# Four global phases, a Strassen step in the second products too, 768-token blocks

## Chip, core, metric

One core of one Trainium2 chip. The metric is the device time of one execution in microseconds (us). Engines: TensorE (PE) multiplies matrices, VectorE (DVE), ScalarE (ACT) and GpSimd (POOL) work element by element, SyncE (SP) issues the DMAs. DRAM tiles are written and read back by DMA.

## What is computed

A linear attention with RMS norm, then two feed-forward layers on 4608 tokens of width 512; all in float32, with weights in float64 words that the kernel converts itself.

```python
kv = einsum('bhsd,bhse->bhde', k, v)          # 8 batches, 8 heads, 576 tokens, 64
out = einsum('bhsd,bhde->bhse', q, kv)
x = out / sqrt(mean(out**2) + 1e-6) * g_norm   # -> [4608, 512]
h = x @ w_in                                   # layer 1: 512 -> 2048
x = (max(h, 0) + alpha * min(h, 0)) @ w_out    # 2048 -> 512
y = ((x @ w_a) * (x @ w_b)) @ w_out2           # layer 2: 512 -> 1536 -> 512
```

## The kernel before

Every operand of the layers is split into two float32r parts, high and low (a `copy` that rounds on ACT, and a subtraction on DVE), and every product is three matmuls: high x low, low x high, high x high.

*First products* (`x @ w_in`, `x @ w_a`, `x @ w_b`): a unit is 256 columns of a weight. One Strassen step (the Winograd form) makes 7 products out of 8 blocks of 256 x 256: `Unit.combine` prepares 7 weight combinations, `X.operands` 7 combinations of a token block of 512 (columns of a matmul: HB = 256). `first` runs a pair of units: 7 products x 2 units x 6 matmuls = 84 matmuls (L583) into the PSUM banks A to D; `copy` (ACT, L598) and `add` (DVE, L602) take the results into H, then the prelu (L624 to L626) or the product a * b (L630), and the split into g (L633 ACT, L634 DVE).

*Second products* (`@ w_out`): `second` multiplies g at once by `WUnit`s, without a Strassen step, 512 columns a matmul (L652), into the four banks acc0 to acc3.

There are four passes over all 9 blocks: half of layer 1 twice, half of layer 2 twice. A pass visits each block with 2 or 3 pairs, each with both products. The first half of a layer stores its partial sums (x2p, outp), the second half loads them and adds (L665, L669). So 90 pairs run, with 7560 matmuls of 256 and 3024 of 512 columns.

*Attention* has 16 steps (`Step`): `kv` (L420, L421), `out` (L437, L442), `norm` (squares L462 on ACT, sums L464, some small instructions on DVE, scaling L481 on POOL), `tr` (transposes L491, L495, then ACT, then a store to xd). Two half-batches make a batch of 576 tokens. The transposes of steps 0 and 1 go from PSUM straight into the first block's operand `xs0.x`. Five steps come ahead, the other 11 one per pair.

*Weights*: `to_float` turns words into float32 (L213 ACT, L214 to L218 DVE, L220 POOL). The first pass's units are converted straight away (`direct`); the others are converted in an earlier pass, stored (`wd`) and loaded again (`build`: `combine` L337, split L295, L296) when a tile of theirs is free.

*Order*: no loop order runs. Every instruction group is a task with a price (COST, AFTER), a priority (a time) and its dependences; `Plan.order` takes for each engine the ready task of lowest priority value, and the kernel is written out in that order. Each engine and the DMA queue of SP work strictly in it.

Of the kernel before, what the change touches and what calls it, by code (L numbers as in the profile page):

```python
# [22 lines left out]
BLK = 512  # L23
CH = 112
NB = TOK // BLK
HB = BLK // 2
EPS = 1e-6

# [5 lines left out]
NFIRST = 5  # L34
AHEAD = 1e6


STEP_AT = [-7.4, -4.8, -4.45, -3.65, -12.5]
X_AT = -0.4
FETCH_AT = [-17.8, -12.9, 7]  # L40
UNIT_AT, WUNIT_AT = [-6.65, -2.75], [0.15, 21.5]

REST_AT, NEXT_X_LOAD, NEXT_X, BUILD, CONVERT = -2, 1.6, -0.3, 6.6, AHEAD
LAST_THREE, SECOND = 0.28, [0.6, 0.1]
SPREAD = [(0, 11), (0, 7), (2, 8)]
# [3 lines left out]
COST = {"v": lambda n: 0.075 + 1.11e-3 * n, "v2": lambda n: 0.075 + 0.556e-3 * n, "a": lambda n: 0.124 + 1.03e-3 * n,  # L49
        "p": lambda n: 0.122 + 2.56e-3 * n, "t": lambda n: n / 2400, "d": lambda n: max(0.5, n / 318e3)}  # L50
AFTER = {"v": 0.13, "a": 0.14, "p": 0.2, "t": 0.2, "d": 2.7}

# [101 lines left out]
def body(ctx: ExitStack, tc, kvm, kvt, qt, gn, w_in, alpha, w_o1, w_a, w_b, w_o2, outT):  # L154
# [24 lines left out]
    x2p = [in_dram([P, 4, BLK], f"x2p{b}") for b in range(NB)]  # L179
    x2d = [in_dram([P, 4, BLK], f"x2d{b}") for b in range(NB)]  # L180
    outp = [in_dram([P, 4, BLK], f"outp{b}") for b in range(NB)]

# [6 lines left out]
    wpool = ctx.enter_context(tc.tile_pool(name="w", bufs=1))  # L189
    spool = ctx.enter_context(tc.tile_pool(name="stg", bufs=1))  # L190
    xpool = ctx.enter_context(tc.tile_pool(name="x", bufs=1))
    hpool = ctx.enter_context(tc.tile_pool(name="h", bufs=1))
# [3 lines left out]
    late = []  # L196

    def sb(pool, shape, tag, n=1, dt=F32):
        return plan.ring(tag, n, lambda key: pool.tile(shape, dt, tag=key, name=key))

    def bank(tag, shape):
        return plan.ring(tag, 1, lambda key: psum.tile(shape, F32, tag=key, name=key))
# [20 lines left out]
    class Built:  # L223


        def __init__(self, w, f0, need):
            self.w, self.f0, self.need, self.closed, self.dram = w, f0, need, False, None

        def take(self):

            n = {"unit": 6, "wu": 4}[self.tag]
            i = plan.counts.get(self.tag, 0)
            plan.counts[self.tag] = i + 1
            key = f"{self.tag}{i % n}"
            self.key = key
            self.pool = (lambda: late[0]) if key in ("unit4", "unit5") else (lambda: wpool)

        def make(self, shape, dt):
            old = plan.rings.get(self.key)
            b = Buf(lambda: self.pool().tile(shape, dt, tag=self.key, name=self.key), old.tasks if old else ())  # L240
            if self.key in ("unit4", "unit5") and not old:
                b.before = list(attention)
            plan.rings[self.key] = b
            return b

        def cuts(self, t, o=0):
# [57 lines left out]
    class Unit(Built):  # L304
# [15 lines left out]
        def place(self):  # L320
            self.c = sb(spool, [P, 8, 2, P], "stg", 2)
# [512 lines left out]
```

## Time and profile before

| | |
|---|---|
| median of 3 runs | 1740.4 us (1740.27 to 1740.61) |
| the profiled execution | 1740.45 us, its span 1738.7 us |
| PE busy | 1695.9 us, 98% |
| DVE busy | 1249.5 us, 72% |
| ACT busy | 769.0 us, 44% |
| POOL busy | 155.0 us, 9% |
| DMA | 195.83 MB, mean 113 GB/s |

The busy time is that of one profiled execution; matmuls overlap in their ends, so the mean duration of one is longer than the distance from one to the next. The chain of waits follows the work that ended last backwards. "L652" is a line of the kernel above.

### The profile page before, as it was taken

The page shows a single profiled execution, that of the slowest core. Times are in us where ns is not written, and L with a number is a line of the kernel's source. Part 1 is how long each engine was busy: PE and PEld are TensorE (multiplying, and loading weights), DVE is VectorE, ACT ScalarE, POOL GpSimd, SP SyncE. Part 2 cuts the span into 40 slices and gives each one's busy share as a digit, 9 for nine tenths or more (in the row PEclk, how much of TensorE's full clock was granted, in tenths as well). Part 3 has the DMA queues.
Part 4 walks back from the last instruction along what each step waited for, and adds up shares of the span by engine and source line. Part 5 has one row for each costly group of instructions (what it writes and reads, how often), then busy time and mean ns, then how long its engine had stood idle before and what let it go on. Part 6 is the DMA issues. An engine that isn't in the chain of part 4 may idle for free.

```text
span 1738.7 us, 28280 instructions
## 1 busy us (share of the span) xinstructions
PE 1695.9 (98%) x11384; PEld 1569.6 (90%) x11384; DVE 1249.5 (72%) x1969; ACT 769.0 (44%) x1315; POOL 155.0 (9%) x110
## 2 busy tenths in 40 slices
PE   4799999999999999999999999999999999999999
PEld 4789989989999999999999999999999999999998
DVE  7997778677667889887786677765577566566654
ACT  4566665665566555555553333333244222222221
POOL 3432122120000001110000111100000000000000
PEclk9899999999999999999999999999999999999999
DMA  9755565442133434443231343321023222221112
GB/s 275 216 167 172 169 204 169 155 145 77 49 96 123 134 122 146 137 135 110 101 114 69 107 134 107 107 98 46 29 85 122 74 74 73 74 66 57 57 41 73
DMA packets 101491, 195.83 MB, mean 113 GB/s; under 512 B 11760, under 2 KB 36336, under 8 KB 99056
## 3 DMA queue, kind: packets, MB, share of 16 engines
q1 hardware_dynamic: 101360, 194.03, 34.3%
q8 instruction: 89, 1.46, 0.3%
q14 instruction: 42, 0.34, 0.1%
HBM read 133.18 MB, written 60.82 MB: 112 GB/s over the span
## 4 chain that ended last, share of the span: by engine, by line
PE 94%; DVE 3%; DMA 1%; issue 1%; SPq 0%; POOL 0%; ACT 0%; POOLq 0%
PE acc L652 39%; PE A L583 15%; PE C L583 15%; PE D L583 14%; PE B L583 7%; PE A L420 1%; PE B L437 1%; DMA kvm<-in_kvm_dram 1%; PE A L437 1%; DMA unit<-in_w_in_dram 0%; PE C L442 0%; DVE H L602 0%; DVE wu L218 0%; PE acc L420 0%; PE A L421 0%
## 5 line engine op out<-in xcount | busy, mean ns | idle before, releaser
L652 PE MATMUL acc<-g,wu 128*128 128x512 f32 x3024 | 714.4, 392 | 3.7 <-DVE g L634 3.7
L652 PEld LDWEIGHTS acc<-g,wu 128*128 128x128 f32 x3024 | 559.1, 188 | 113.4 <-DVE g L634 4.3
L583 PE MATMUL D<-xc,unit 128*128 128x256 f32 x2160 | 291.1, 284 | 5.1 <-DVE xc L568 3.6
L583 PE MATMUL A<-xc,unit 128*128 128x256 f32 x2160 | 289.8, 284 | 0.0
L583 PE MATMUL C<-xc,unit 128*128 128x256 f32 x2160 | 288.2, 283 | 0.3 <-DVE H L602 0.3
L583 PEld LDWEIGHTS A<-xc,unit 128*128 128x128 f32 x2160 | 278.7, 192 | 7.4
L583 PEld LDWEIGHTS D<-xc,unit 128*128 128x128 f32 x2160 | 272.2, 191 | 5.8 <-DVE xc L568 3.8
L583 PEld LDWEIGHTS C<-xc,unit 128*128 128x128 f32 x2160 | 271.4, 191 | 1.6 <-DVE H L602 0.7
L598 ACT COPY H<-A 128x512 f32<-128x512 f32 x180 | 105.2, 585 | 337.7 <-PE A L583 330.4
L633 ACT CAST g<-H 128x512 fp32r<-128x512 f32 x252 | 155.5, 622 | 208.3 <-DVE H L630 119.5
L634 DVE TENSOR_TENSOR g<-H,g 128x512 fp32r<-128x512 f32 x252 | 183.2, 734 | 48.0 <-ACT g L633 45.2
L602 DVE TENSOR_TENSOR H<-H,C 128x512 f32<-128x512 f32 x180 | 123.4, 686 | 81.6 <-PE C L583 77.0
L568 DVE TENSOR_TENSOR xc<-xf,xc 128x512 fp32r<-128x512 f32 x143 | 104.0, 730 | 88.9 <-ACT xc L567 88.0
L567 ACT CAST xc<-xf 128x512 fp32r<-128x512 f32 x144 | 89.1, 620 | 166.1 <-PE A L583 111.1
L602 DVE TENSOR_TENSOR H<-H,B 128x512 f32<-128x512 f32 x90 | 61.7, 686 | 119.4 <-PE B L583 119.1
L220 POOL TENSOR_TENSOR stg<-stg 128x512 f32<-128x512 f32 x52 | 74.8, 1438 | 805.3 <-DVE stg L218 521.7
L602 DVE TENSOR_TENSOR H<-H,D 128x512 f32<-128x512 f32 x180 | 123.2, 685 | 31.8 <-PE D L583 25.4
L583 PE MATMUL B<-xc,unit 128*128 128x256 f32 x1080 | 143.6, 282 | 0.0
L626 DVE SCALAR_TENSOR_TENSOR H<-H,nal_sb,t 128x512 f32<-128x512 f32 x144 | 116.7, 810 | 34.1 <-ACT H L625 34.0
L583 PEld LDWEIGHTS B<-xc,unit 128*128 128x128 f32 x1080 | 135.3, 191 | 0.0
L624 ACT ACTIVATE t<-H 128x512 f32<-128x512 f32 x144 | 90.8, 631 | 74.5 <-DVE H L626 39.0
L625 ACT ACTIVATE H<-H 128x512 f32<-128x512 f32 x144 | 90.8, 630 | 2.4
(94 smaller groups left out, 1227.5 us busy)
## 6 DMA issues: line engine op xcount, KB each, us to landing
xf<-x2d SPq DMA_DIRECT2D x18, 1024.0 KB, 4.8
kvm<-in_kvm_dram SPq DMA_DIRECT2D x32, 448.0 KB, 5.9
wd<-stg SPq DMA_DIRECT2D x52, 256.0 KB, 2.2
stg<-in_w_o_dram SPq DMA_DIRECT2D x20, 512.0 KB, 4.0
q<-in_qt_dram SPq DMA_DIRECT2D x32, 288.0 KB, 3.8
x2p<-y SPq DMA_DIRECT2D x36, 256.0 KB, 2.5
y<-x2p SPq DMA_DIRECT2D x36, 256.0 KB, 4.3
x2d<-y SPq DMA_DIRECT2D x36, 256.0 KB, 2.1
```

Of the source, the lines that this page charges most:

```text
L220: task("p", n, lambda: nc.gpsimd.tensor_add(out(), permute(f32(a())), permute(f32(u()))), prio, [A, U], [dst])
L567: task("a", 512, lambda c=c, v=v: nc.scalar.copy(c.t[:, 0], v()), prio, r, [(c, 0)])
L568: sub(512, lambda e, c=c, v=v: e.tensor_sub(c.t[:, 1], v(), f32(c.t[:, 0])), prio, r + [(c, 0)], [(c, 1)])
L583: nc.tensor.matmul(bk.t[:, u], w[:, a, i, kk, :], c[:, b, kk, :], start=bool(new and u == 0 and kk == 0 and m == 0), stop=(kk == 1 and m = ...
L598: task("a", 512, lambda: nc.scalar.copy(H.t[:, :, q], bk.t), k, [(bk, 0), (bk, 1)], [(H, (0, q)), (H, (1, q))])
L602: task("v", 512, lambda: nc.vector.tensor_add(H.t[:, :, q], H.t[:, :, p], bk.t), k, [(bk, 0), (bk, 1), (H, (0, p)), (H, (1, p))], [(H, (0, ...
L624: task("a", 512, lambda t=t, v=v: nc.scalar.activation(t.t, v(), AF.Relu), pk, pv, [(t, 0)])
L625: task("a", 512, lambda v=v: nc.scalar.activation(v(), v(), AF.Relu, scale=-1.0), pk, pv, pv)
L626: task("v", 512, lambda t=t, v=v, nal=nal: nc.vector.scalar_tensor_tensor(v(), v(), nal, t.t, ALU.mult, ALU.add), pk, pv + [(t, 0)], pv)
L633: task("a", 512, lambda g=g, v=v: nc.scalar.copy(g.t[:, 0], v()), pk, pv, [(g, 0)])
L634: sub(512, lambda e, g=g, v=v: e.tensor_sub(g.t[:, 1], v(), f32(g.t[:, 0])), pk, pv + [(g, 0)], [(g, 1)], "v")
L652: nc.tensor.matmul(a_.t, w.h.t[:, a, i % 2, d * P:(d + 1) * P], g.t[:, b, :], start=(start and m == 0), stop=(stop and m == 2))
```

## The change

Layer by layer, all first products of all blocks run, and then all second products: four phases. In between, g stands in DRAM (`gd`), unsplit; partial sums x2p and outp are gone. First products take blocks of 768 tokens (6 blocks; matmuls of 384 columns) and use five PSUM banks, each group of six matmuls writing one bank; two banks gather two or three products, so ACT copies 8 and DVE adds 6 results of 384 columns per pair. Layer 1's first phase visits six blocks with four pairs of units each, but begins with three pairs of blocks 0, 1 and 2 (list `V`); layer 2's goes over the blocks twice with three pairs. Second products take 512 tokens (9 blocks) and units of 256 rows, by a Strassen step: per unit two loads from `gd`, four differences of 256 columns (L599), one split of 1,792 columns (L605 ACT, L606 DVE), 7 x 6 = 42 matmuls of 256 columns (L613). Each of the seven products gathers over all units in a bank of its own; after the last unit one copy and seven sums on DVE (L626) make the block's four quarters. So there are 5040 matmuls of 384 and 5292 of 256 columns.

The buffers share memory: a token block lies in F0, H in F1 and F2, and in the second phases these three hold the loaded g; `rops` holds the seven split operands of a block, or three units of g. All units lie in eight tiles w0 to w7; w6 and w7 lie where attention's buffers were, and are first written after attention's last instruction. Six units are converted at the start (w0 to w5, three pairs). Four attention steps come ahead; two more go with each of the first six pairs. Transposes always go through xd, and q has two buffers and not three. Splits and differences go to DVE alone.

```diff
-BLK = 512
+T1ST, N1 = 768, 384
+T2ND, N2 = 512, 256
-NFIRST = 5
+NFIRST = 4
...
-    x2p = [in_dram([P, 4, BLK], f"x2p{b}") for b in range(NB)]
-    outp = [in_dram([P, 4, BLK], f"outp{b}") for b in range(NB)]
+    gd = [[in_dram([P, 2, TOK], f"gd{la}_{u}") for u in range(n)] for la, n in ((0, 8), (1, 6))]
...
+    SLOTS = [f"w{i}" for i in range(8)]
+    def slot(key, shape, dt):
+        old = plan.rings.get(key)
+        b = Buf(lambda: (late[0] if key in SLOTS[6:] else pool).tile(shape, dt, tag=key, name=key),
+                old.tasks if old else (attention if key in SLOTS[6:] else ()))
...
+    def first(k, la, units, js, x):
...
+        for u in range(2):
+            copy(u, 0, X_[u], prod(u, 0, X_[u], 1))
+        for u in range(2):
+            prod(u, 2, Y_[u], 1)
+            copy(u, 1, X_[u], prod(u, 1, X_[u], 0))
+        for u in range(2):
+            Z_[u] = bank("b4", [P, 512])
+            add(u, 0, Z_[u], prod(u, 4, Z_[u], 1))
+            t = prod(u, 3, X_[u], 0)
+            copy(u, 3, X_[u], t)
+            add(u, 3, Y_[u], t)
+        for u in range(2):
+            copy(u, 2, X_[u], prod(u, 6, X_[u], 0))
+            add(u, 1, Y_[u], prod(u, 5, Y_[u], 0))
...
+    ORDER = [0, 1, 3, 6, 2, 5, 4]
+
+    def second(k, la, b, j, n, unit, bk):
+
+        g, t0 = gd[la][j], b * T2ND
+        s = sb(["F0", "F1", "F2"], [P, 8, N2])
...
+        for i, o in enumerate((lambda: s.t[:, 0::7], lambda: s.t[:, 4:6])):
+            dma(262144, o, lambda i=i: g.t[:, i, t0:t0 + T2ND].rearrange("p (h t) -> p h t", h=2), k - 16,
...
+        for o, a, c in ((t1, b12, b11), (t2, b22, t1), (t3, b22, b12), (t4, b21, t2)):
+            sub(N2, lambda e, o=o, a=a, c=c: e.tensor_sub(s.t[:, o[0]], s.t[:, a[0]], s.t[:, c[0]]), k - 7,
...
+        c = rop((plan.counts.setdefault("gx", 0) % 3) * 14 * N2, 14 * N2)
...
+        task("a", 7 * N2, lambda: nc.scalar.copy(half(0), s.t[:, 0:7]), k - 7, reads, [(c, 0)])
+        sub(7 * N2, lambda e: e.tensor_sub(half(1), s.t[:, 0:7], f32(half(0))), k - 7, reads + [(c, 0)], [(c, 1)], "v")
...
+        copy(0, 0)
+        add(1, 0, 1)
+        add(2, 1, 3)
+        add(3, 2, 2)
+        add(2, 2, 6)
+        add(1, 1, 2)
+        add(1, 1, 5)
+        add(0, 0, 4)
...
+    V = [(0, 0, [0, 1, 2]), (0, 1, [0, 1, 2]), (0, 2, [0, 1, 2, 3]), (0, 0, [3]), (0, 3, [0, 1, 2, 3]), (0, 1, [3]),
+         (0, 4, [0, 1, 2, 3]), (0, 5, [0, 1, 2, 3])]
+    V += [(0, b, None) for b in range(NB2)]
+    V += [(1, b, [3 * h, 3 * h + 1, 3 * h + 2]) for h in range(2) for b in range(NB1)]
+    V += [(1, b, None) for b in range(NB2)]
```

How PE's order stands where attention runs among the products, before (L420, L421 are kv, L437 the output, L491 and L495 the transposes of a step; L583 and L652 products):

```order
L491 MATMUL B<-ident,o_120 128x112 x4
L420 MATMUL A<-kvm_2828 128x128 x4
L421 MATMUL A<-kvt_2848 128x128
L420 MATMUL A<-kvm_2858 128x128 x4
L421 MATMUL A<-kvt_2871 128x128
L583 MATMUL C<-xc_2826,unit_267 128x256 x6
L583 MATMUL D<-xc_2856,unit_240 128x256 x6
L437 MATMUL A<-kvbd,q_2762 112x128 x4
L491 MATMUL C<-ident,o_120 128x112 x4
L583 MATMUL D<-xc_2856,unit_267 128x256 x6
L652 MATMUL acc_2653<-g_2904,wu_1244 128x512 x3
L652 MATMUL acc_2660<-g_2904,wu_1244 128x512 x3
```

Between two pieces of attention stand products. In the changed kernel this is so for nine visits of pairs; then, at the end of attention (L276 kv of step 15, L346 and L350 transposes, L292 and L297 the output, L537 a first product; w_2789 is unit 6):

```order
L276 MATMUL b_2657<-kvt_2555 128x128
L346 MATMUL b_2705<-ident,o_108 128x112 x4
L346 MATMUL b_2715<-ident,o_108 128x112 x4
L350 MATMUL b_2720<-ident,o_108 128x128 x2
L292 MATMUL b_2723<-kvbd,q_2680 112x128 x4
L292 MATMUL b_2733<-kvbd,q_2685 112x128 x4
L297 MATMUL b_2740<-kvbd,q_2680 128x128
L297 MATMUL b_2740<-kvbd,q_2685 128x128
L346 MATMUL b_2764<-ident,o_109 128x112 x4
L346 MATMUL b_2771<-ident,o_109 128x112 x4
L350 MATMUL b_2776<-ident,o_109 128x128 x2
L537 MATMUL b_2795<-rops,w_2789 128x384 x6
```

The transposes of step 14, the output of step 15 and its transposes follow one another without a product between them, and the next product reads unit 6.

DVE's order late in the kernel before, about one pair of layer 2 (L602 results of the first products, L630 and L634 g, L337 and L296 a unit being built):

```order
L602 TENSOR_TENSOR H_12885<-H_12885,B 128x2x256
L602 TENSOR_TENSOR H_12885<-H_12885,C 128x2x256
L602 TENSOR_TENSOR H_12885<-H_12885,D 128x2x256
L337 TENSOR_TENSOR stg_12901<-stg_12901 128x256 x2
L602 TENSOR_TENSOR H_12885<-H_12885,C 128x2x256
L337 TENSOR_TENSOR stg_12901<-stg_12901 128x256
L630 TENSOR_TENSOR H_12885<-H_12885 128x512
L602 TENSOR_TENSOR H_12885<-H_12885,D 128x2x256
L337 TENSOR_TENSOR stg_12901<-stg_12901 128x256
L634 TENSOR_TENSOR g_12974<-H_12885,g_12974 128x512
L630 TENSOR_TENSOR H_12885<-H_12885 128x512
```

The same engine in the changed kernel in layer 1's second products, where a block ends:

```order
L606 TENSOR_TENSOR rops<-F_5753,rops 128x1792
L599 TENSOR_TENSOR F_5841<-F_5841 128x256
L606 TENSOR_TENSOR rops<-F_5779,rops 128x1792
L626 TENSOR_TENSOR y_5900<-t,b_5471 128x512
L599 TENSOR_TENSOR F_5841<-F_5841 128x256
L626 TENSOR_TENSOR y_5917<-y_5900,b_5479 128x512
L626 TENSOR_TENSOR t<-t,b_5490 128x512
L626 TENSOR_TENSOR y_5934<-y_5917,b_5515 128x512
L626 TENSOR_TENSOR y_5900<-y_5900,b_5515 128x512
L626 TENSOR_TENSOR y_5917<-y_5917,b_5507 128x512
L626 TENSOR_TENSOR y_5900<-y_5900,b_5526 128x512
L599 TENSOR_TENSOR F_5841<-F_5841 128x256 x2
```

The seven sums of a block stand together, between the subtractions (L606) and differences (L599) that the next units wait for.

More of the change, by code (lines that the diff above doesn't have):

```diff
@@ L187, in body @@
     nal_sb = const.tile([P, DF1 // P], F32, name="nal_sb")
[L189 to L192, printed above, removed]
+    pool = ctx.enter_context(tc.tile_pool(name="main", bufs=1))
     psum = ctx.enter_context(tc.tile_pool(name="ps", bufs=1, space=bass.MemoryType.PSUM))
@@ new lines, in body @@
+    attended(lambda: steps[NFIRST - 1].tr(TR0))
+    for i in range(3, 6):
+        us1[i].fetch(SLOTS[i], 25.0 + 8 * (i - 3))
+        owner[SLOTS[i]] = us1[i]
+    x = X(0, 0)
+    x.load(26.0)
+    x.operands(32.0)
+    for i in range(6):
+        us1[i].direct(us1[i].need - 6, 2 if i < 2 else 1)
+    rest = us1[6:] + wo1 + [u for p in us2 for u in p] + wo2
+    rest.sort(key=lambda u: u.need)
+    convs, builds = list(rest), list(rest)
+    due = {}
+    for i, u in enumerate(rest):
+        if u in us1:
+            due[u] = START + 40 + 25 * i
+        elif u in wo1:
+            due[u] = START + 140 + 25 * wo1.index(u)
+        elif u in wo2:
+            due[u] = wo1[0].need + 420 + 40 * wo2.index(u)
+        else:
+            due[u] = wo1[0].need + 8 + 32 * (rest.index(u) - rest.index(us2[0][0]))
@@ new lines, in body @@
+    end = None
+    pending = [i for i in sorted(at_time)]
+    trq = []
+    for pi, (vi, j, t) in enumerate(pieces):
+        la, b, ps = V[vi]
+        fst = pi == 0 or pieces[pi - 1][0] != vi
+        if ps is not None:
+            units = (pairs1, us2)[la][j]
+            end = first(t, la, units, [2 * j, 2 * j + 1] if la == 0 else [j], x)
+        else:
+            n = 8 if la == 0 else 6
+            units = [(wo1, wo2)[la][j]]
+            if fst:
+                bk = [bank(f"b{i}", [P, 2, N2]) for i in range(7)]
+            end = second(t, la, b, j, n, units[0], bk)
+        for u in units:
+            if last[u] == pi:
+                u.closed = True
+        if pi + 1 < len(pieces) and pieces[pi + 1][0] != vi and V[vi + 1][2] is not None:
+            x = X(V[vi + 1][0], V[vi + 1][1])
+            tn = pieces[pi + 1][2]
+            x.load(tn - 30)
+            x.operands(tn - 9)
+        for i in [i for i in pending if at_time[i] == pi]:
+            pending.remove(i)
+            attend(i, t + 6.0 * (i % 2) - 4)
+            st = steps[-1]
+            attended(lambda: st.kv("b7"))
+            if trq:
+                p_ = trq.pop()
+                attended(lambda: p_.tr(TR0))
+            attended(lambda: (st.out(TR0), st.norm()))
+            trq.append(st)
+        if not pending and trq:
+            p_ = trq.pop()
+            attended(lambda: p_.tr(TR0))
+        while convs and due[convs[0]] <= t:
+            u = convs.pop(0)
+            u.convert(t + CONVERT, [end])
+        while builds and builds[0] not in convs:
+            u = builds[0]
+            free = [s for s in SLOTS if (s in owner and owner[s].closed) or
+                    (s not in owner and not pending and not trq)]
+            if not free:
+                break
+            key = min(free, key=lambda s: last[owner[s]] if s in owner else -1)
+            u.build(key, u.need - BUILD)
+            owner[key] = u
+            builds.pop(0)
@@ L782, in body @@
+    assert not convs and not builds
     make_identity(nc, ident)
```

688 lines of the change are left out of this document (294 added, 394 removed).

## The prediction

> **What bounds the kernel now.** I read the chain of waits first, then the time by stage.
>
> ```profile
> PE 94%; DVE 3%; DMA 1%; issue 1%; SPq 0%; POOL 0%; ACT 0%; POOLq 0%
> PE acc L652 39%; PE A L583 15%; PE C L583 15%; PE D L583 14%; PE B L583 7%; PE A L420 1%; PE B L437 1%; DMA kvm<-in_kvm_dram 1%; PE A L437 1%; DMA unit<-in_w_in_dram 0%; PE C L442 0%; DVE H L602 0%; DVE wu L218 0%; PE acc L420 0%; PE A L421 0%
> ```
>
> TensorE's matmuls are 94% of the chain: second products (L652) 39%, first products (L583) 51%. The stages show where that holds (columns: stretch, length, then busy time of each engine with its instructions, granted clock, DMA share, GB/s):
>
> ```profile
> core 0: us, PE busy (x) PEld busy (x) DVE busy (x) ACT busy (x) POOL busy (x), PEclk, DMA share, GB/s
> 0.00:40.00 40.00, 19.36 (x110) 18.00 (x110) 31.26 (x55) 16.56 (x26) 13.45 (x17) 0.96 0.95 276
> 80.00:120.00 40.00, 34.77 (x238) 32.09 (x237) 37.79 (x65) 25.30 (x50) 14.66 (x10) 0.91 0.56 183
> ...
> 700.00:800.00 100.00, 100.00 (x642) 91.36 (x641) 88.04 (x137) 54.66 (x95) 10.07 (x7) 1.00 0.47 153
> 660.00:680.00 20.00, 20.00 (x125) 17.99 (x125) 19.18 (x29) 12.63 (x22) 3.01 (x3) 1.00 0.57 191
> ```
>
> PE is idle only at the start. Later it is full, even where VectorE (DVE) is 88% busy, and for 20 us 96%. So what counts is PE time per product, PE's idle start, and whether DVE stays under PE. The price of a matmul comes from the chain in order of time (start, length):
>
> ```profile
> 1631.28 5.47 PE acc L652 x24
> 1677.70 5.47 PE acc L652 x24
> 1724.12 10.92 PE acc L652 x48
> ```
>
> 24 matmuls of 512 columns take 5.47, so 0.2279 us each. The block between the first two rows is 46.42 us long and holds 3 x 24 of these and 3 x 84 of 256 columns: (46.42 - 16.41)/252 = 0.1191 each. The last ends at 1735.04, 3.7 us before the span's end: the tail. All products are 7560 x 0.1191 + 3024 x 0.2279 = 1589.6 us. Attention on PE:
>
> ```profile
> 10.89 2.07 PE L420 MATMUL acc<-kvm 112*128 112x128 f32 x8 [10.89 <-DMA kvm<-in_kvm_dram]
> ...
> 56.30 1.63 PE L583 MATMUL A<-xc,unit 128*128 128x256 f32 x6
> ...
> 69.56 2.67 PE L583 MATMUL D<-xc,unit 128*128 128x256 f32 x12 [3.61 <-DVE xc L568]
> ...
> 76.59 0.55 PE L491 MATMUL acc<-ident,o 112*128 112x112 f32 x4
> 76.98 0.39 PE L495 MATMUL acc<-ident,o 128*128 128x128 f32 x2
> 77.20 1.06 PE L420 MATMUL A<-kvm 112*128 112x128 f32 x8
> ...
> 78.31 1.04 PE L437 MATMUL acc<-kvbd,q 128*112 128x128 f32 x8
> 79.19 1.06 PE L420 MATMUL A<-kvm 112*128 112x128 f32 x8
> ...
> 80.31 0.61 PE L442 MATMUL acc<-kvbd,q 128*128 128x128 f32 x4
> 80.67 0.95 PE L583 MATMUL C<-xc,unit 128*128 128x256 f32 x6
> ...
> 118.85 0.61 PE L442 MATMUL C<-kvbd,q 128*128 128x128 f32 x4
> ```
>
> From start to start: a kv half 1.11, an output half 0.88, the rest of the output 0.36, a transposed half 0.39, the last transposes 0.22. A step is 2 x (1.11 + 0.88 + 0.39) + 0.36 + 0.22 = 5.34 us, 16 steps 85.4. Span 1738.7 less products and attention leaves 63.7 us of idle and slow clock.
>
> **The change, part by part.** The sum is against the span; the profiled execution took 1740.45, 1.75 more, and agrees with the median of 1740.4.
>
> *Products.* First products: 60 block-and-pair visits x 84 = 5040 matmuls of 384 columns, a width without a row. Bounds by proportion: 384/512 x 0.2279 = 0.1709 and 384/256 x 0.1191 = 0.1787. I take the mean of the two rows, 0.1735, since 384 lies midway: 874.4 us. Second products: 126 unit visits x 42 = 5292 of 256 columns, 630.3. Sum 1504.7, which is 84.9 less than now; 13 less or 26 more at the bounds.
>
> *Start.* Now the first product runs at 56.30, once two steps are done, from an operand that the transposes write directly. Afterwards a block takes 768 tokens, so steps 0 to 3 must pass through DRAM first. Before that load the queue carries four steps (1.77 MB each), five units of raw weights and stores, some 13.5 MB: at the 276 GB/s of the first row 49 us from about 4. Then the second part of the load, one difference, one cast and one subtraction: steady products from about 74 us (69.56 now). PE's work until then is four steps, a kv and two products, 25.6: idle 48, with ends 40 and 64 (a start at 90, if step 3 is held up by weight conversions as today).
>
> *Nine visits and twelve steps, then a gap.* PE's new order has 9 visits (131 us) mixed with steps 4 to 15; it then has no product until units 6 and 7 are built, whose tiles lie where attention's buffers were. The last transposes, output, norm and transposes stand one after the other. Price of a norm:
>
> ```profile
> L462 ACT ACTIVATE sq<-o 128x640 f32<-128x640 f32 x32 | 23.7, 740 | 5.2 <-DVE sm L464 5.1
> L464 DVE TENSOR_REDUCE sm<-sq 128x10 f32<-128x640 f32 x32 | 26.0, 812 | 10.6 <-ACT sq L462 10.4
> ```
> ```profile
> 131.07 2.93 POOL L481 TENSOR_TENSOR o<-o,sm 128x640 f32<-128x640 f32 x2 [7.33 <-DVE sm L476]
> ```
>
> From the output of 118.85 (end 119.46) to the scaling at 131.07 it takes 11.6 under load; two squares and one sum alone are 2.3. I take 8, with the engines emptier, plus 2.9 for the scalings. Step 14: 8 + 2.9 + 0.6 = 11.5; copies and output of step 15: 2.7; its norm and transposes 11.5; cast and subtraction of 1,792 columns, by L296's row below 2 each: 4. About 30, less PE's own 6.3 and some 4 of overlapping halves: idle 20, ends 8 and 27. I add 6 for waits inside the nine visits. After pauses the clock is low:
>
> ```profile
> 50.00:55.00 5.00, 2.58 (x11) 2.23 (x12) 4.94 (x6) 0.63 (x1) 5.00 (x4) 0.50 1.03 243
> 55.00:60.00 5.00, 5.00 (x28) 5.00 (x27) 5.00 (x11) 2.55 (x7) 1.66 (x1) 0.53 0.79 273
> ```
>
> Half clock over some 5 us of work after each of three pauses, with little PE work in two: 4 us. The Trainium skill (TensorE: Matmul & The Clock Gate, "Part 1: The HAM clock gate") says that about 3.4 us without matmuls brings the half clock back, for about 3.4 us. That speaks against a change that opens a gap; by its figures three pauses cost 5 us, one more than my sum has, and the two rows agree.
>
> *DVE.* The prices (busy, mean ns) and the spacing:
>
> ```profile
> L602 DVE TENSOR_TENSOR H<-H,C 128x512 f32<-128x512 f32 x180 | 123.4, 686 | 81.6 <-PE C L583 77.0
> L626 DVE SCALAR_TENSOR_TENSOR H<-H,nal_sb,t 128x512 f32<-128x512 f32 x144 | 116.7, 810 | 34.1 <-ACT H L625 34.0
> L215 DVE SCALAR_TENSOR_TENSOR stg<-stg 128x512 int32<-128x512 int32 x52 | 45.5, 875 | 1.1
> L218 DVE SCALAR_TENSOR_TENSOR stg<-stg 128x512 f32<-128x512 uint32 x52 | 37.7, 725 | 1.0
> L296 DVE TENSOR_TENSOR unit<-stg,unit 128x1792 fp32r<-128x1792 f32 x18 | 36.4, 2022 | 3.4 <-ACT unit L295 3.2
> L337 DVE TENSOR_TENSOR stg<-stg 128x256 f32<-128x256 f32 x80 | 33.5, 433 | 1.6 <-POOL stg L220 1.2
> L214 DVE TENSOR_SCALAR stg<-stg 128x512 int32<-128x512 int32 x52 | 24.7, 475 | 19.4 <-ACT stg L213 18.8 <-DMA wd<-stg 0.4
> L217 DVE TENSOR_SCALAR stg<-stg 128x512 int32<-128x512 int32 x52 | 23.7, 455 | 0.7
> ```
> ```profile
> 53.78 1.75 DVE L568 TENSOR_TENSOR xc<-t,xc 128x512 fp32r<-128x512 f32 x1
> ...
> 59.88 0.68 DVE L562 TENSOR_TENSOR xf<-xf 128x512 f32<-128x512 f32 x1
> 60.48 0.68 DVE L562 TENSOR_TENSOR t<-xf,t 128x512 f32<-128x512 f32 x1
> ```
> ```profile
> 53.27 1.71 POOL L220 TENSOR_TENSOR stg<-unit 128x512 f32<-128x512 f32 x1
> ```
>
> Neighbours start 0.60 apart and last 0.68, so 0.08 of each overlaps. Second products of layer 1: per unit four differences of 256 (L337) and one subtraction of 1,792 (L296), 3.75; 72 units are 270. With 56 sums of 512 (38), ten weight conversions (20 halves at 2.53, 51) and 12 of remainder: 371, less 0.08 on 505 instructions: 331. PE needs 360.5. Beside a POOL addition a DVE instruction took 1.75 and not 0.69; 20 such additions fall here: 21 more at most, 352. That is 92 to 98%, in the order of the 88 and 96% above where PE lost nothing: I put 4 us of waits, ends 0 and 31 (392 without overlap). The 15 last visits of layer 1's first products are tighter: 55 prelu instructions of 768 columns (1.5 x 0.810), 8 conversions, 7 builds and the operands are 234, less 23 for overlap, up to 16 for POOL: 211 to 227 against 218.6 of PE. I put 8, ends 0 and 31. Layer 2's first products have 426 against 525, its second 249 against 270: no loss. ACT has 116 instructions against DVE's 505 in the second products: hidden under DVE.
>
> *Borders, DMA, tail.* Between first and second products, the last prelu, its store and the new operand share ACT and DVE: one more chain of cast (2.0) and subtraction (2.0) stands bare: 5 us; the other two borders together 3. Intermediate g goes through DRAM, 66 MB each way, and the partial sums leave it: in the second products 0.52 MB per 5 us and the rest, some 175 GB/s, under the 276 of the first row. Tail 4, as now.
>
> Sum: 1504.7 + 85.4 + idle (48 + 6 + 20 + 4 + 8 + 5 + 4 + 3 + 4 = 102) = 1692 of span, **1694 us**.
>
> **Rivals.** *DVE becomes the bound.* For it: the high ends above, 250 against 218.6 and 392 against 360.5, and every new DVE instruction has two inputs. Against it: 96% in the row of 660 to 680 with PE at 20.00. Halfway to the high ends it is +25, 1719; at the ends +50, 1744. The Trainium skill (SBUF — State Buffer, "Who interferes with whom") says that a DVE instruction with two SBUF inputs and a GpSimd instruction that reads SBUF lock each other out for a whole instruction; the rows of 53.27 and 53.78 agree. By it 20 additions of 1.71 would take 34, not 21, from DVE: 365 against 360.5, 5 us more in my sum.
>
> *Attention sets the early time.* Its start at 90 and norms of 11.6: +16 and +7, 1717; a little more with waits between steps, 1725. For it: norms of 11.6 under load. Against it: conversions now come behind attention.
>
> *The operand loop of the second products sets the pace (slower than before).* Three tiles F hold a unit each from load to subtraction:
>
> ```profile
> y<-x2p SPq DMA_DIRECT2D x36, 256.0 KB, 4.3
> ...
> wu<-in_w_o_dram SPq DMA_DIRECT2D x8, 512.0 KB, 8.7
> ```
>
> Load 4.3, four differences 1.4, cast and subtraction 4: 9.7, and three tiles cover 3 x 5.0 = 15. It decides above 15, and those 5.3 us also cover a load that stands on SP's queue behind the store of a converted weight half, which waits for POOL. From a loop of 16.1 (0.37 more on each of 126 units, 46 us) the kernel is slower than now: a load of 10.7. At 12 us the loop is 17.4, 5.8 a unit: +100, 1794. Against it: 4.3 for the same size, and 8.7 only for twice the size in the crowded start.
>
> *384 columns cost 0.1787*: +26, 1720.
>
> **How the numbers follow.** Forecast as worked out (1660 to 1715) 0.60; DVE 0.20; attention 0.10; operand loop 0.06; width 0.04. The range 1660 to 1735 reaches low to a short gap and no waits (-12 - 18), high to the DVE case short of its end. Within 0.2% (3.5 us, about what this kernel's runs can tell apart) 0.03, the edge of the DVE case; slower 0.09: the loop, and DVE at its end; faster 0.88.
>
> **What would show it.** Right: 384-column matmuls spaced 0.173 and 256-column 0.119; steady products from 74 us; a hole of 20 to 25 us with four attention pieces near 270 to 290; PE near 100% and DVE 90% and more in the second products. Wrong: PE waiting for the F tiles' subtractions all along, or DVE at 100% with PE below 95%.

## The result, and the profile after

The changed kernel takes 1834.55 us (median of four; three lie at 1830.25 to 1834.58) where the kernel before takes 1740.34: a ratio of 1.0534, 95% interval 1.0513 to 1.0554. It is 5.3% slower; forecast were 1694 us and a gain. One execution took 4375 us and one of the last version below 2060 us, for reasons that stay open: no ratio counts them, and as the profiler recorded the first, the profile after is of a second run of the same kernel.

> The changed kernel once more, unchanged, for a profile of an ordinary execution (the profiled one took 4375 us with matmuls of 256 columns 0.298 us apart; the others 1830 to 1835 us at a granted clock of 0.952). Theory 1 (the granted clock): matmuls stand closer than before and PE is nearly always busy, but the clock falls below 1.00 for long stretches; 0.048 of 1832 us, some 88 us, is lost there, and the rest of the time is near my sum. Theory 2 (waits): the low mean clock is only that of pauses, PE is idle for 100 us and more beyond the 102 that I counted, in the first products of layer 1 or the second products, where DVE or the operand loop is late. Theory 3 (width): a matmul of 384 columns costs more than 0.1787 us at clock 1.00.

It took 1830.53 us (ratio 1.0522, interval 1.0504 to 1.0540). Its chain of waits, by engine and by line:

```profile
PE 80%; DVE 11%; ACT 3%; issue 3%; DMA 2%; POOL 0%; SPq 0%; DVEq 0%; ACTq 0%; POOLq 0%
PE b L537 45%; PE b L613 32%; PE b L292 2%; DVE rops L606 1%; DVE F L576 1%; PE b L275 1%; DVE rops L505 1%; DVE w L460 1%; DVE stg L451 1%; PE b L346 1%; ACT w L458 1%; DVE F L599 1%; ACT t L574 1%; DMA kvm<-in_kvm_dram 1%; DVE F L547 1%
```

PE was 94% of the chain and is 80%. No single line takes its place: some fifteen lines have about 1% each. That is the picture of many different waits, not of one new bound. The unbroken stretches of the chain give the price of the products (start, length, matmuls):

```profile
629.86 266.56 PE b L613 x2230
...
1036.17 279.74 PE b L537 x1601
...
1320.64 223.11 PE b L537 x1284
...
1563.23 258.48 PE b L613 x2172
```

384 columns cost 279.74/1601 = 0.1747 and 0.1738 us, 256 columns 0.1195 and 0.1190. With 0.174 and 0.1192 all products are 877.0 + 630.8 = 1507.8 us; forecast were 1504.7. The saving in matmuls is there in full. The loss is in the rest, and the stages tell where. I cut at the first product, the end of attention, the first second product, layer 2's first product and its first second product (columns: stretch, length, busy time of each engine with its instructions, clock, DMA share, GB/s):

```profile
core 0: us, PE busy (x) PEld busy (x) DVE busy (x) ACT busy (x) POOL busy (x), PEclk, DMA share, GB/s
0.00:71.20 71.20, 33.09 (x191) 30.96 (x191) 45.27 (x89) 29.96 (x54) 24.38 (x24) 0.80 0.83 255
71.20:319.50 248.30, 214.91 (x1365) 209.60 (x1366) 172.06 (x301) 166.56 (x295) 50.95 (x33) 0.91 0.61 202
319.50:592.20 272.70, 234.56 (x1246) 227.73 (x1244) 214.10 (x303) 189.48 (x294) 24.02 (x16) 0.93 0.48 169
592.20:983.20 391.00, 368.81 (x3043) 366.59 (x3043) 339.14 (x512) 149.50 (x115) 51.57 (x20) 0.97 0.52 170
983.20:1543.60 560.40, 534.46 (x3027) 530.35 (x3026) 397.28 (x576) 237.89 (x405) 23.62 (x16) 0.97 0.35 123
1543.60:1828.80 285.20, 271.85 (x2269) 271.24 (x2267) 219.76 (x331) 93.45 (x62) 0.00 (x0) 0.98 0.41 131
```

Lost is a stage's length less its matmuls at the prices above (and 85.4 for attention). Third row: 272.70 - 1246 x 0.174 = 55.9. The last column is the best version of the experiments, shown at their end.

| stage | work, after | lost, forecast | lost, after | lost, last version |
|---|---|---|---|---|
| start and attention | 216 | 78 | 103 | 86 |
| last 15 visits of layer 1's first products | 217 | 8 | 56 | 19 |
| border and second products, layer 1 | 364 | 9 | 27 | 14 |
| border and first products, layer 2 | 526 | 2 | 34 | 7 |
| border, second products, tail | 270 | 5 | 15 | 16 |
| sum | 1593 | 102 | 235 | 142 |

Of the 235 us PE stands idle for 1828.8 - 1657.7 = 171 (the span less the busy time of all stages), where 98 were forecast. In the other 64 it works, but slower than the price. The slow clock is enough for that: the granted clock of the stages is 0.80 to 0.98, and their busy times, each times what its clock lacks to 1, sum to some 75 us, an estimate from these rounded figures. So of the three theories ahead of this run, waits have the larger part and the clock the rest; a dear matmul has none. Some rows of PE alone (stretch, length, busy time, clock, DMA share, GB/s), then the matmuls behind three pauses, which stand in brackets:

```profile
416.00:418.50 2.50, 2.33 (x13) 1.00 0.28 112
452.00:456.00 4.00, 4.00 (x15) 0.58 0.35 100
475.00:478.00 3.00, 3.00 (x10) 0.50 0.86 292
511.00:514.00 3.00, 3.00 (x10) 0.50 0.75 250
```
```profile
416.17 4.44 PE L537 MATMUL b<-rops,w 128*128 128x384 f32 x24 [2.29 <-ACT F L544]
451.75 17.46 PE L537 MATMUL b<-rops,w 128*128 128x384 f32 x90 [2.36 <-ACT F L544]
508.95 1.31 PE L537 MATMUL b<-rops,w 128*128 128x384 f32 x6 [2.42 <-ACT F L544]
```

After the pause of 2.29 us the clock is full. After one of 5.59 us (shown below) PE runs at half clock for some 5 us (the next 16 matmuls take 5.38 us and not 2.8): the pause is paid twice. But pauses of 2.36 and 2.42 us, with shorter ones close by (1.16 and 1.05 us before the one, 0.47 after the other), end in 3 us of half clock too. The Trainium skill (TensorE: Matmul & The Clock Gate, "Part 1: The HAM clock gate") gives about 3.4 us as the idle time that brings the half clock. The pauses of 2.29 and 5.59 us agree with that and those of 2.36 and 2.42 us do not; here the measurement decides.

**The start.** PE alone, cut where the steady products begin and around the hole at attention's end:

```profile
0.00:95.39 95.39, 49.63 (x290) 0.80 0.76 231
95.39:295.90 200.51, 190.55 (x1226) 0.96 0.66 218
295.90:324.38 28.48, 8.94 (x43) 0.61 0.28 111
```

Steady products come at 95 us and not at 74. But PE is busy for 49.6 us before them and not for 25.6, so it idles for 45.8 us there, then for 10.0 and 19.5; forecast were 48, 6 and 20. The excess of this stage is slow work: of its 103 us, 319.5 - 33.1 - 214.9 = 71.5 are idle, and some 31 are work above the price.

**The 15 visits.** PE's waits between 319.5 and 592.2 (in all, times, longest), and then the microseconds before one of them, that of 474.80, on ACT, DVE and PE:

```profile
PE b L537 <- ACT F L544: 26.0, 10, 5.6
PE b L537 <- DVE rops L505: 6.7, 3, 3.9
```
```profile
467.93 0.85 ACT L574 ACTIVATE t<-F 128x768 f32<-128x768 f32 x1 [2.12 <-DVE F L576]
468.81 0.84 ACT L575 ACTIVATE F<-F 128x768 f32<-128x768 f32 x1
...
473.54 0.84 ACT L574 ACTIVATE t<-F 128x768 f32<-128x768 f32 x1 [0.53 <-DVE F L576]
474.29 0.46 ACT L544 COPY F<-b 128x384 f32<-128x384 f32 x1
```
```profile
465.84 2.06 DVE L576 SCALAR_TENSOR_TENSOR F<-F,nal_sb,t 128x768 f32<-128x768 f32 x1 [0.18 <-ACT F L575]
469.68 1.02 DVE L576 SCALAR_TENSOR_TENSOR F<-F,nal_sb,t 128x768 f32<-128x768 f32 x1 [1.79 <-ACT F L575]
```
```profile
474.80 0.69 PE L537 MATMUL b<-rops,w 128*128 128x384 f32 x1 [5.59 <-ACT F L544]
```

Each relu (L574) writes the only tile `t` and so waits for the L576 of the quarter before; L576 in turn waits for ACT (L575). The two engines hand work back and forth, both with idle time between. The copy that empties PE's bank (L544) stands behind in ACT's order and comes 5 us late. ACT is busy for 69% of this stage, DVE for 79%: neither is full.

**The borders.** From first to second products PE waits twice; at the border to layer 2 it waits for units being built (its waits from 983.2 to 1543.6), and SP's queue shows a reason:

```profile
611.07 7.64 PE L613 MATMUL b<-rops,w 128*128 128x256 f32 x42 [10.48 <-DVE rops L606]
627.78 1.44 PE L613 MATMUL b<-rops,w 128*128 128x256 f32 x5 [9.07 <-DVE rops L606]
```
```profile
PE b L537 <- ACT w L458: 14.4, 2, 13.7
```
```profile
994.18 0.37 SPq L166 DMA_DIRECT2D stg<-in_w_a_dram  x1
...
1005.95 0.33 SPq L166 DMA_DIRECT2D wd<-stg  x1
...
1011.64 0.60 SPq L166 DMA_DIRECT2D stg<-wd  x1
```

At 994.18 a conversion's words are loaded into `stg`, at 1005.95 the converted half is stored, and only at 1011.64, 28 us into the stage, is the next load of a unit (`stg<-wd`) issued.

### The profile page after: what moved, and what is told of

The parts are those of the page before. It is cut to its first block, busy times and chain, and to the rows that moved or that the text cites. A ratio compares the mean times of both kernels' runs of the same rounds, so it can differ in the third digit from the quotient of the medians.

```text
span 4373.4 us, 28430 instructions
## 1 busy us (share of the span) xinstructions
PE 4277.4 (98%) x11132; PEld 3691.1 (84%) x11132; DVE 1383.6 (32%) x2108; ACT 879.4 (20%) x1223; POOL 148.4 (3%) x109
## 4 chain that ended last, share of the span: by engine, by line
PE 97%; DVE 1%; ACT 1%; issue 1%; DMA 0%; POOL 0%; SPq 0%; ACTq 0%; DVEq 0%; POOLq 0%
PE b L537 54%; PE b L613 36%; PE b L275 2%; PE b L292 2%; PE b L346 1%; PE b L276 1%; PE b L297 1%; PE b L350 0%; DVE rops L606 0%; DMA stg<-wd 0%; ACT rops L605 0%; DVE w L460 0%; DVE stg L451 0%; ACT w L458 0%; DVE sm L319 0%
## 5 line engine op out<-in xcount | busy, mean ns | idle before, releaser
L537 PE MATMUL b<-rops,w 128*128 128x384 f32 x5040 | 2403.9, 713 | 42.3 <-DVE rops L505 18.5
L537 PEld LDWEIGHTS b<-rops,w 128*128 128x128 f32 x5040 | 1821.3, 364 | 586.0 <-issue 473.3
L613 PE MATMUL b<-rops,w 128*128 128x256 f32 x5292 | 1577.4, 529 | 25.1 <-DVE rops L606 25.1
L613 PEld LDWEIGHTS b<-rops,w 128*128 128x128 f32 x5292 | 1575.9, 444 | 26.9 <-DVE rops L606 26.2
L547 DVE TENSOR_TENSOR F<-F,b 128x384 f32<-128x384 f32 x360 | 198.8, 553 | 1236.8 <-PE b L537 924.4
L544 ACT COPY F<-b 128x384 f32<-128x384 f32 x480 | 229.1, 478 | 1521.8 <-PE b L537 1505.1
L606 DVE TENSOR_TENSOR rops<-F,rops 128x1792 fp32r<-128x1792 f32 x126 | 255.0, 2024 | 809.2 <-ACT rops L605 809.1
L605 ACT CAST rops<-F 128x1792 fp32r<-128x1792 f32 x126 | 212.6, 1688 | 1194.9 <-PE b L613 963.5
L599 DVE TENSOR_TENSOR F<-F 128x256 f32<-128x256 f32 x504 | 187.5, 427 | 7.9 <-DMA F<-gd 6.8
L505 DVE TENSOR_TENSOR rops<-F,rops 128x768 fp32r<-128x768 f32 x120 | 114.6, 964 | 150.8 <-ACT rops L504 142.4
L576 DVE SCALAR_TENSOR_TENSOR F<-F,nal_sb,t 128x768 f32<-128x768 f32 x96 | 98.8, 1029 | 153.7 <-ACT F L575 153.5
L275 PE MATMUL b<-kvm 112*128 112x128 f32 x256 | 113.7, 674 | 6.1 <-DMA kvm<-in_kvm_dram 4.7
L292 PE MATMUL b<-kvbd,q 128*112 128x128 f32 x256 | 109.9, 672 | 3.1 <-issue 2.3
L292 PEld LDWEIGHTS b<-kvbd,q 128*112 128x112 f32 x256 | 101.7, 443 | 12.4 <-issue 8.4
L574 ACT ACTIVATE t<-F 128x768 f32<-128x768 f32 x96 | 81.1, 845 | 53.6 <-DVE F L576 30.5
L575 ACT ACTIVATE F<-F 128x768 f32<-128x768 f32 x96 | 81.0, 843 | 1.0
L626 DVE TENSOR_TENSOR y<-y,b 128x512 f32<-128x512 f32 x67 | 44.4, 683 | 82.5 <-PE b L613 82.5
```

Of the source, the lines that this page charges most:

```text
L275: nc.tensor.matmul(ps.t[:, s], m[:, 0, c, :], m[:, 1, c, :], start=(c == 0), stop=False)
L292: nc.tensor.matmul(p[s].t[0:CH, t, :], self.q[s].t[:, t * CH:(t + 1) * CH], self.z.t[:, s], start=True, stop=True)
L505: sub(n, lambda e: e.tensor_sub(w(1), v(), f32(w(0))), prio, a[1] + [(c, 0)], [(c, 1)], "v")
L537: nc.tensor.matmul(bk.t[:, 0:N1], w.h.t[:, a, i, kk, :], ct[:, b, kk, :], start=bool(new and kk == 0 and m == 0), stop=(kk == 1 and m == 2 ...
L544: task("a", N1, lambda: nc.scalar.copy(H.t[:, u, q], bk.t[:, 0:N1]), t, [(bk, 0)], [(H, (u, q))])
L547: task("v", N1, lambda: nc.vector.tensor_add(H.t[:, u, q], H.t[:, u, q], bk.t[:, 0:N1]), t, [(bk, 0), (H, (u, q))], [(H, (u, q))])
```

## Experiments

All times are compared with the 1830.5 us of the unchanged version.

**1. A second tile for the prelu.**

```diff
-                    r = place("t", [P, T1ST])
+                    r = place(("t", "T1")[s], [P, T1ST])
```

> The prelu's copy r gets two tiles in turn (t and T1) instead of one; nothing else. In the unchanged version the 15 last visits of layer 1's first products took 283 us where PE needs 219. Theory A (ACT's strict order): the relu of L574 waits for L576 to free the only tile t, and the copies out of PSUM (L544) stand behind it, so PE waits for a bank. Then a second tile gives back 15 to 30 of these 64 us, and the time is 1800 to 1815. Theory B (DVE has too much to do there): DVE's work is the same, nothing moves, 1827 to 1833. Theory C (384-column matmuls suffer themselves): nothing moves either.

1815.35 us, 15 less. The visits take 264.2 us and lose 264.2 - 1263 x 0.174 = 44, some 11 less than without:

```profile
318.60:582.80 264.20, 234.70 (x1263) 229.41 (x1263) 207.54 (x288) 189.25 (x294) 25.06 (x16) 0.93 0.48 170
```
```profile
PE b L537 <- DVE rops L505: 20.7, 8, 4.8
PE b L537 <- DVE F L547: 5.0, 6, 1.5
```

(Second fence: PE's waits in this stage.) No wait for ACT's L544 is left, though ACT has as much to do as before; most of it became a wait for DVE's splits (L505). Theory A is right on the place, and its gain is at the low end: 15 us in all, 11 of them here. The single tile was one link of the loss; what stands behind it the next experiment tells.

**2. The prelu in one instruction.**

```diff
-                    task("a", T1ST, ... AF.Relu), t, pv, [(r, 0)])
-                    task("a", T1ST, ... AF.Relu, scale=-1.0), t, pv, pv)
-                    task("v3", ... v(), v(), nal, r.t, ALU.mult, ALU.add), t, pv + [(r, 0)], pv)
+                    task("v3", ... v(), v(), al, v(), ALU.mult, ALU.max), t, pv, pv)
```

> The prelu is one DVE instruction, max(x, alpha x), which is the same for alpha up to 1 (here it is at most 0.3); both relu passes of ACT (192 x 0.85 = 163 us) are gone and DVE keeps its 96 instructions of 768 columns. Theory A (ACT's order and the hand-overs between ACT and DVE delay the copies out of PSUM): most of the 64 us goes, some 10 us of the attention visits too, 1765 to 1790. Theory B (DVE's sum of work is the bound there): DVE is as busy as before, 1820 to 1833. Between them (1790 to 1820) both have a share.

1786.63 us, 44 less, the most of any single edit:

```profile
314.50:551.80 237.30, 225.31 (x1262) 223.59 (x1260) 191.53 (x279) 100.69 (x179) 25.08 (x16) 0.97 0.53 188
```

The visits lose 237.3 - 1262 x 0.174 = 18 instead of 56, though DVE has its 96 prelu instructions still. What cost was the prelu's way over ACT. The edit takes away the passing to and fro and ACT's work of 163 us at once; that the passing is what counts follows for the single tile from experiment 1, and for the rest it is argued from ACT being busy for only 69%. Of the 44 us, 35 are gained in the visits and 6 in those that attention is mixed with. Another 8 are in layer 2's first products (552.7 instead of 560.4), which have no prelu: the order of the whole program is written anew for every edit, and a stage that the edit does not touch can move by that much.

**3. The same edit in the kernel before.**

> The kernel before the change with the one-instruction prelu, nothing else. It has one tile t as well, and the same three instructions in a row. Theory A (before, second products of the same pass stand ready for PE while the prelu runs, so its waits are covered): no change, 1736 to 1742. Rival (the prelu's waits cost there too, and the gain in the changed kernel tells nothing about the change): 1700 to 1730.

1741.52 against 1739.49 us (ratio 1.0014, interval 1.0005 to 1.0022): nothing gained. Its page:

```profile
PE 1694.8 (98%) x11384; PEld 1567.8 (90%) x11384; DVE 1238.4 (71%) x1969; ACT 608.8 (35%) x1027; POOL 154.1 (9%) x110
```

ACT is spared 160 us (769.0 before), and PE is 98% busy either way. The kernel before has the same three instructions and one tile `t`, and no wait to lose: in its passes second products stand between the first products. In four global phases that cover is gone. That the second products are the cover is argued from the order; that the prelu's waits cost nothing there is shown.

**4. Conversions spaced 40 us.**

```diff
-            due[u] = wo1[0].need + 8 + 32 * (rest.index(u) - rest.index(us2[0][0]))
+            due[u] = wo1[0].need + 8 + 40 * (rest.index(u) - rest.index(us2[0][0]))
```

> Conversions of layer 2's first weights are spaced 40 us and not 32, so that the last four come after the border to layer 2 instead of right ahead of it. At that border (985 to 1036 us) PE has 51 us for 28 us of work at a low clock, some 30 to 35 us lost. Theory A: the loads that rebuild layer 2's units need the two tiles stg, which conversions written into the order ahead of them still hold; then the border loses 10 to 15 and the time is 1800 to 1812. Theory B: the eight weight tiles become free too late, as the last block uses them all; then the border stays as it is and the time is 1826 to 1833. The stall at 900 to 946 should shrink by either, if conversions are behind it.

1804.39 us, 26 less. The stage of layer 2's first products:

```profile
980.30:1518.80 538.50, 528.99 (x3026) 527.37 (x3025) 394.16 (x578) 236.60 (x405) 27.45 (x19) 0.99 0.38 131
```

It loses 12 instead of 34. Eight weight tiles are in use as before, so they were not what was late; the loads were, behind conversions that held the two tiles `stg`, as theory A has it. The second part of the expectation fell: in the second products only 3 us were gained. Of the 27 us that the unchanged version loses in that stage the two pauses at the border are 20, so there was little left to gain; the stall at 900 to 946 that the expectation speaks of is a detour of the chain over DVE, during which PE hardly waited.

**5. The last addition of a conversion on DVE.**

```diff
-        task("p", n, lambda: nc.gpsimd.tensor_add(out(), permute(f32(a())), permute(f32(u()))), prio,
+        task("v", n, lambda: nc.vector.tensor_add(out(), permute(f32(a())), permute(f32(u()))), prio,
```

> The last addition of each weight conversion (L241) runs on DVE instead of POOL: 56 additions, about 0.69 each, 38 us more work for DVE, and no POOL instruction beside DVE after attention. Theory A (POOL and DVE hold each other up: L241 took up to 8.8 us, L576 2.06 instead of 1.01 beside it, and the store of the sum then blocks SP's queue): the stall at 900 to 946 goes, the 15 visits lose less, 1795 to 1820. Theory B (DVE simply has too much to do in these stages): each addition costs its time, 1835 to 1860. Near 1830 both cancel.

1818.79 us, 12 less: 257.0 instead of 272.7 in the visits, 396.2 instead of 391.0 in the second products. That seemed to speak for theory A, and so do L576's durations in the visits (min/median/max), unchanged version first, then this one:

```profile
L576 DVE SCALAR_TENSOR_TENSOR F<-F,nal_sb,t x55: 1003/1012/2055, 344.3 to 588.4; 128x768 f32<-128x768 f32 x55
```
```profile
L576 DVE SCALAR_TENSOR_TENSOR F<-F,nal_sb,t x56: 1006/1014/1020, 348.8 to 580.7; 128x768 f32<-128x768 f32 x56
```

Without POOL beside it none takes 2 us any more. But the next experiment contradicts that this is where the 12 us came from.

**6. No conversions of the stored weights.**

```diff
-                to_float(raw, a, u, ...)
+                task("a", 512, ... nc.scalar.copy(self.fit(o()), self.permute(f32(raw()[:, :, :, 1]))), ...)
```

> The 28 weight conversions that are stored for later (56 halves) are left out but for one copy on ACT each; loads, stores and tiles stay, so the weights are wrong. DVE is spared 56 x 2.5 = 140 us, POOL 106 us. Theory A (the 15 last visits of layer 1 wait for ACT's and DVE's order about the prelu, and border 2 for the two tiles stg): the visits still lose 40 or more of their 56, border 1 loses as before, border 2 falls from 34 to 10 or less, time 1785 to 1800. Theory B (DVE's sum of work): the visits fall to 15 lost, border 1 to under 10, time 1745 to 1765. The POOL share shown by moving the additions to DVE was 16 us in the visits.

1790.72 us. Visits, and first products of layer 2 (the second products between them take 385.3 us):

```profile
310.80:585.40 274.60, 236.46 (x1251) 231.23 (x1250) 177.48 (x242) 190.65 (x294) 0.00 (x0) 0.91 0.48 169
...
970.70:1506.90 536.20, 530.81 (x3026) 528.34 (x3025) 354.01 (x506) 234.99 (x401) 0.00 (x0) 0.99 0.35 125
```

In the visits DVE is spared 37 us, POOL does nothing, and they lose 57 us, as much as ever. PE's waits there for ACT's L544 are 30.0 us (26.0 before). So neither DVE's sum of work nor POOL at its side makes that loss. What the fifth experiment gained there came, then, most likely with the order, which the planner writes anew for every edit; a small gain may hide behind a worse order here, theory B's 40 us could not. Border 2 falls to 536.2 - 526 = 10, by another way than in the fourth experiment: with no conversions to compute, `stg` is soon free.

**7. The last prelu left out.**

```diff
-                if la == 0:
+                if la == 0 and (x.b, js[u]) not in ((5, 6), (5, 7)):
```

> The prelu of the very last pair of layer 1's first products (block 5, units 6 and 7: 8 ACT and 4 DVE instructions) is left out, and its products are stored as they are. At the border to the second products PE lost 24.6 us (592 to 630). Theory A (a chain through memory: the tiles F1 and F2 that the second and third g unit are loaded into hold that pair's and the pair before's results until prelu and store are done; then load, differences and split follow one after the other): the chain is some 8 to 10 us shorter, time 1815 to 1823. Theory B (DVE's backlog, eight weight units to build at 3.7 us each while the pair runs): DVE is spared 4.4 us only, 1825 to 1830.

1817.16 us, 13 less. The second products of layer 1 take 380.1 us, 11 less, and PE's waits in them (was 21.5 in all), with what is left of the border's two pauses:

```profile
PE b L613 <- DVE rops L606: 11.9, 4, 10.2
```
```profile
610.65 39.61 PE L613 MATMUL b<-rops,w 128*128 128x256 f32 x309 [10.23 <-DVE rops L606]
```

Four DVE instructions are 4.4 us, so DVE's backlog alone does not give 13. The second pause (9.07 us, ahead of the third unit) is gone, and for it the chain of theory A fits: prelu, store, load into the tile that was stored, differences, split. Its single links were not tested. The first pause (10.48, now 10.23 us) stays without that prelu; what makes it stays open.

**8. Short conversions at the start.** Units 2 to 5 get one ACT copy per half instead of `to_float`.

> The four units 2 to 5 that are converted at the start get one copy on ACT per half in place of the conversion, so their weights are wrong; DVE is spared 8 x 2.5 = 20 us between about 35 and 130 us. Steady products began at 95 us, forecast 74. Theory A (DVE's conversions delay attention's steps 2 and 3, whose norm needs small DVE instructions in turn, and so the load of the first block's second part, issued at 85.8): steady products from 78 to 86, the time 10 to 17 shorter, 1813 to 1820. Theory B (SP's queue and the loads set it): steady products at 93 to 96, 1826 to 1832.

1814.70 us, 16 less; attention ends at 303.8 and not 319.5:

```profile
0.00:68.00 68.00, 32.67 (x191) 30.61 (x191) 39.66 (x82) 33.39 (x57) 19.78 (x21) 0.83 0.88 259
68.00:303.80 235.80, 208.11 (x1366) 201.82 (x1366) 157.88 (x276) 161.49 (x293) 42.62 (x28) 0.96 0.65 215
```

20 us less work for DVE, 16 us less time: the conversions cost something here. Whether by DVE's work or by the order that was written anew is not shown, as the second experiment's 8 us warn. The place was other than expected: steady products began at 97.6 us, no earlier than without. 3 us were gained ahead of the first product and 12.5 in the visits that attention is mixed with, where PE's idle time fell from 33 to 28 us and the clock rose from 0.91 to 0.96.

**9. Edits together.** Short prelu and spacing 40, with `NFIRST = 6` and layer 1's second weights due at `START + 100`:

> One-instruction prelu (worth 44 us alone), conversions of layer 2 spaced 40 us (worth 26 alone), six attention steps ahead instead of four, and layer 1's second weights converted 40 us earlier. If the losses are separate, as theory A has it (each stall has its own cause and place), the gains add: 1830 less 70 less 10 to 18 for the two last edits, 1740 to 1752, about the time of the kernel before. If they hide one another (rival: one common bound, DVE), the sum is short: 1765 to 1785.

1743.69 us, 87 less (ratio to before 1.0022, interval 1.0012 to 1.0032). Prelu and spacing alone are 44 and 26. The two large gains stand side by side: the visits take 237.3 us, as with the prelu alone, and layer 2's first products 537.6, as with the spacing alone (538.5), so these two stalls were separate. The prelu's 8 us in layer 2 do not add to that. The rest, 15 us up to attention's end (5 with the prelu alone) and 14 in layer 1's second products (376.7 instead of 391.0, where the prelu alone gave 393.7 and the spacing alone 387.8), must come for the most part from the two other edits or from the order; those edits were not run singly. The time lies in theory A's range. Then more due times and priorities were moved, so that the kernel's own planner ends earlier; and the additions went to DVE, in all conversions after attention, and last only in those made in the visits:

> The version with everything together, with more of its times and priorities moved (conversions of layer 1's last first weights and of its second weights earlier still, operands earlier, second-product operands later); no instruction is added or left out. Theory A (what is left are stalls from the order of the written-out program, about 80 us over the forecast's products and attention): 10 to 18 us are gained, 1724 to 1734, faster than the kernel before by 0.4 to 0.9%. Rival (the rest is DVE's work and the fixed chains at start and borders): 1740 to 1746, no change.

> As the version with moved times (some of them set anew), and every weight conversion after attention does its last addition on DVE instead of POOL, so that no POOL instruction runs beside DVE there. Alone on the unchanged version this gave 12 us, 16 of them in the 15 last visits. Theory A (POOL and DVE hold each other up there, whatever the prelu does): 5 to 12 us less than the version with moved times, 1715 to 1726. Theory B (with the short prelu DVE has slack for being held up, and the 40 additions cost their 28 us in the second products): 0 to 10 us more.

> As the version with moved times and additions on DVE, but only the conversions of layer 1's second weights (made in the 15 last visits) do their last addition on DVE; those in the second products and later do it on POOL again, and two times are as in the version with moved times. Theory A (the held-up DVE matters where DVE and ACT work for each product, and not in the second products, where the additions only add DVE work and delayed the border to layer 2 by 6 us): start and visits as in that version, border 2 as in the other, 1728 to 1736. Rival (what is left is fixed chains and pauses): 1737 to 1743, no change.

1741.41 (1.0011, 1.0002 to 1.0019), 1739.28 (1.0001, 0.9992 to 1.0009) and 1737.54 us (0.9982, 0.9973 to 0.9991). Moving times alone gave 2 us, not 10 to 18: the rival was right there. With the additions on DVE (and some times set anew) it was another 2 us, less than the 5 that theory A asked for, as the sixth experiment lets expect. The last version is 0.2% faster than the kernel before, about as little as can be told from no change, and its time lies where its rival, not theory A, put it:

```profile
0.00:75.60 75.60, 42.97 (x250) 40.84 (x250) 47.22 (x91) 35.45 (x63) 23.65 (x24) 0.84 0.83 250
75.60:298.20 222.60, 199.40 (x1283) 193.45 (x1283) 174.66 (x301) 110.37 (x216) 57.80 (x37) 0.95 0.69 230
298.20:539.10 240.90, 227.58 (x1275) 224.79 (x1272) 206.41 (x305) 106.39 (x180) 6.34 (x2) 0.97 0.51 184
539.10:915.70 376.60, 365.25 (x3037) 363.57 (x3037) 336.65 (x517) 144.05 (x107) 63.30 (x18) 0.99 0.53 172
915.70:1449.80 534.10, 527.18 (x3027) 525.83 (x3026) 394.52 (x578) 236.81 (x405) 27.15 (x19) 1.00 0.38 132
1449.80:1736.30 286.50, 273.22 (x2269) 272.60 (x2267) 219.79 (x331) 93.54 (x62) 0.00 (x0) 0.99 0.41 130
```

It still loses 142 us, 40 more than the forecast: mostly at the start, in the visits and at the two borders to second products. Which part of that a better order could give back stays open.

## Why the prediction was wrong, point by point

- *Products*: right. 1507.8 us measured, 1504.7 forecast. The rival of a dear 384-column matmul fell.
- *Start and attention*: 78 us of idle and slow clock forecast, 103 measured. The idle time came out right (71.5 us, forecast 74), in part by luck: steady products come 21 us later than forecast, but PE has 24 us more work before them. What failed here is the term for the slow clock, 4 us, where some 31 are work above the price. The time of steady products was worked out from the loads alone. DVE, which converts weights and serves the norm's small steps, is busy for 64% ahead of the first product, but sparing it 20 us did not bring them forward (experiment 8); what holds the first block's second part back stays open. The hole was sized right, with 19.5 us of idle time. The rival that attention sets the early time had the late start right and the size of the excess, but by idle time (64 us ahead of the steady products, measured 45.8) and long norms, which is not what came.
- *The 15 last visits*: the step that failed most. 8 us, with ends 0 and 31, came from comparing DVE's sum (211 to 227) with PE's 218.6. DVE's sum was sized well (214.1 busy in the stage), yet 56 were lost. A sum says whether an engine can keep up, not whether it does in a fixed order with a hand-over inside. "96% in the row of 660 to 680 with PE at 20.00" spoke of a pass with other work for PE in between. The prediction priced the prelu by DVE's part alone and never looked at ACT's order in this stage. What stood in its place is shown by experiments 1 and 2: the prelu's way over ACT lost 38 of the 56 us, some 11 of them by its single tile, though no engine was full.
- *Borders*: 5 + 3 forecast; the three stages with a border lost 76 us in place of 16. A border was priced as one more bare cast and subtraction. Of layer 1's two pauses one fits a chain through a tile and DRAM (experiment 7) and one stays open; at layer 2 it is a queue for `stg` (experiment 4). The prediction looked at neither.
- *Slow clock*: 4 forecast; 64 us of work above the price measured. The size for one pause was right (some 5 us at half clock after 5.59 us of idle time). But there were many pauses, not three, and some of 2.4 us brought the half clock too.
- *"Layer 2's first products: no loss"*, second products: right away from the borders (2885 matmuls in two unbroken stretches; 0.1190 to 0.1195 with DVE at 339.14/391.00 = 87%). The rival of a DVE bound fell: sparing DVE 140 us (experiment 6) left the visits as slow. So did that of the operand loop: 2230 matmuls of second products stand in one stretch of 266.56 us without a wait.
- *The range*: its high end took DVE's bound as the worst case but for the operand loop. But for attention's and the operand loop's, no rival had waits without a full engine, and none had them in the visits, where they came.

## What to carry to other kernels

Where a change parts work that used to run side by side into phases, look at each short wait that the other work covered: the same prelu's way over ACT costs nothing in the mixed kernel and some 40 us in the phased one. Price such a stage by following one item through the engines in their written order (who frees the tile, who stands behind the waiting instruction), since totals of 70 to 80% on ACT and DVE left room here for a fifth of the time to be lost. Count each pause of PE with the slow clock that can follow it, and each border between phases as a chain of its own.

## What the runs showed of the hardware

A pause of 2.29 us left PE's clock full and one of 5.59 us halved it for some 5 us, but pauses of 2.36 and 2.42 us with shorter ones near them also led to 3 us of half clock; the length of one pause does not decide it alone, and what does stays open. Over the whole kernel 171 us of idle time went with some 64 us of slower work. DVE's two-input instruction of 768 columns took up to 2.06 us with POOL beside it and at most 1.02 without, and two POOL additions, each 1.36 us in the median, stretched to 10.04 us together:

```profile
909.68 10.04 POOL L241 TENSOR_TENSOR stg<-stg 128x512 f32<-128x512 f32 x2 [28.82 <-DVE stg L239]
```

The Trainium skill (SBUF — State Buffer, "Who interferes with whom") has the two engines lock each other out, and these rows agree; unexpected was that taking POOL away altogether (experiment 6) did not shorten the visits at all.
